# A chunked RWKV-5 attention with a squared-relu FFN on one core: 47 transfers issued by ScalarE's queue, nine transposes moved from DMA to TensorE, and a new order of the steps

## The chip, the core and the metric

The kernel runs on one core of a Trainium2 chip. The core has TensorE (PE, matrix products and transposes into PSUM), VectorE (DVE), ScalarE (ACT), GpSimd (POOL) and SyncE (SP), each with an instruction queue of its own that it works off in order, and 16 DMA engines that the queues of SyncE, ScalarE and GpSimd hand transfers to. The metric is the device time of one execution in microseconds, the median of several runs.

## The reference

```python
B, H, S, D = 4, 8, 768, 48
state = zeros((B, H, D, D))
for t in range(S):
    cur = einsum('bhd,bhe->bhde', u[None] * k[:, :, t], v[:, :, t])
    y[:, :, t] = einsum('bhd,bhde->bhe', r[:, :, t], state + cur)
    state = w[None, :, :, None] * state + einsum('bhd,bhe->bhde', k[:, :, t], v[:, :, t])
x = y.transpose(0, 2, 1, 3).reshape(B * S, H * D)      # 3072 x 384
h = maximum(x @ w_in, 0)                               # 3072 x 2048
return h * h @ w_out                                   # 3072 x 384
```

Everything is fp32 outside; the kernel multiplies in bf16.

## The kernel before

The recurrence is done in chunks of 128 tokens. A unit is one batch and one chunk, all eight heads together: 4 x 6 = 24 units, numbered in the order in which they are worked. For one unit the steps are, by the names that the order uses:

- `ld.r`, `ld.k`, `ld.v` (L312): load r, k, v, 128 tokens x 384 numbers of fp32. The first four units are paired: `lp` (L316) loads two units at once, each row of the tile two neighbouring tokens.
- `rh`, `kh` (L335, L332): multiply r and k by powers of w (tables `Wt`, `Wk`, made once from w) into the bf16 tile `rk`.
- r and k transposed, so that tokens lie along the free dimension (tile `rkT`): either by TensorE (`T`, L393, eight transposes into a PSUM bank, then the copy `Tc`) or by a DMA transpose (`XB`, L399). For the paired units TensorE does it (`TK`, `TR`, copies `KC`, `RC`).
- `A` (L406, paired `Ap` L379): scores of k against r; `Bm` (L414, paired `Bp`): times the causal mask.
- `P0`, `P1`, `du`, `dv` (L338, L342, L345, L350): the term of the token itself, sum over d of r k u, times v. `vb` casts v to bf16.
- `U` (L458): k times v, the chunk's share of the state; `ts` adds it to the old state and `S` (L479) scales by the decay (`S0` for the first chunk).
- `Y` (L445, L447; paired L423 to L435): r times the state plus masked scores times v; `xs` (L470) adds `dv`: this is x of the unit, 128 x 384 bf16.
- x transposed (tile `xT`): by TensorE (`X`, L484, three transposes into PSUM, then the copy `xTc`) or by a DMA transpose (`xX`, L491).

The FFN then runs over groups, units 0 and 1 alone and after that two units at a time (13 groups). `F1.g.s` (L500) is one bank of h of group g (6 matmuls for a group of two units, 12 for a group of one), `re` (L508 on ScalarE, L510 on VectorE) the relu into bf16, `sq` (L515, L517) the square. `F2.i.q` (L526) adds four of the 16 slices of d_ff to unit i's output bank; `os` (L256, L258) brings the bank to SBUF and `out` (L554, L556) stores it. `Z.n` (L535) are n columns-blocks of products of the identity with itself into a spare bank, which nothing reads; four blocks go into one matmul. `lW` and `W` load w_in and w_out, `cW` casts w_in.

The order of all steps is written out by hand as a string, `ORDER`. A step reads `name.unit:engine/slots`, the engine being P (TensorE), D (VectorE), A (ScalarE), G (GpSimd) or S (SyncE's queue, for transfers). Each engine receives its steps in that order and works them off in that order; a buffer's slot is given behind the slash, and the waits between engines follow from tiles and slots. So a transfer that is listed behind another on the same queue is issued behind it, and a wait holds up what is queued behind it. In the kernel before, all loads of r, k, v and all stores are on SyncE's queue, together with the 34 DMA transposes; ScalarE's queue issues only w, u and the two small column loads `wc`.

Of the kernel before, what the change touches and what calls it, by code (L numbers as in the profile page):

```python
# [26 lines left out]
Z.23:P/2 Ap.0.1:P/2/3 dv.1:G vb.2:A/2 WLcol:A du.0:D/1 TK.1:P/4 KC.1:A/2 Bp.0.1.1:D/0 Ap.0.0:P/5/6 rh.3:G/3  # L27
Bp.0.1.0:D/1 Bp.0.0.0:D/2 U.3:P/7 WLm:G vb.1:A/3 Z.10:P/0 U.0:P/0 cW.1:A rh.2:D/2 dv.0:G Bp.0.0.1:D/3 TR.1:P/1 cW.0:A
U.2:P/4 S0.0:D Y.0:P/3 RC.1:A/3 P0.2:D/2 lW.3:S/0 Y.1:P/2 ld.r.5:S/4 P0.3:G/3 P1.3:G S0.2:D ts.3:D/0 ld.k.5:S/4
xs.0:A/0 X.0:P/5 xs.1:A/1 Ap.1.0:P/6/0 Bp.1.0.1:D/4 xTc.0:A/0 Ap.1.1:P/1/4 cW.2:G cW.3:A X.1:P/7 F1.0.0:P/3 ld.k.4:S/5  # L30
xTc.1:D/1 W.1:G Wt.2:A P1.2:D F1.1.1:P/2 du.3:D/2 cW.5:A cW.4:G F1.1.0:P/5 du.2:D/3 re.1.1:A/0 re.0.0:A/1 Bp.1.0.0:D/5
ld.r.4:S/5 F1.0.1:P/7 dv.3:G Bp.1.1.1:D/6 F1.1.2:P/2 dv.2:G ld.v.5:S/4 re.0.1:A/2 Bp.1.1.0:D/7 F1.0.2:P/3 W.0:G cW.7:D
re.1.2:A/3 Y.2:P/7 cW.6:G re.1.0:D/4 Y.3:P/2 Wk.2:A ld.k.6:S/6 xs.2:A/2 re.0.2:D/5 sq.1.1:D/0 sq.1.0:D/1 W.2:G X.2:P/5
W.3:G F1.0.3:P/7 xs.3:A/3 xTc.2:D/0 sq.0.0:A/2 X.3:P/3 ld.r.6:S/6 F1.1.3:P/2 rh.5:D/4 xTc.3:A/0 re.0.3:A/0 re.1.3:A/4
U.1:P/5 F1.2.6:P/3 ts.1:D/1 P0.5:D/4 sq.0.1:D/3 sq.0.3:A/4 F1.2.3:P/7 kh.5:D/4 P1.5:G F1.2.1:P/2 F1.2.2:P/5 re.2.6:A/1
sq.0.2:A/5 sq.1.3:D/6 rh.4:D/5 S.3:G kh.4:G/5 F2.1.1:P/3 du.5:D/4 F2.1.0:P/3 re.2.3:A/2 P0.4:G/0 P1.4:D re.2.1:A/0
re.2.2:A/5 F2.0.0:P/7 ld.v.4:S/5 F1.2.0:P/2 sq.1.2:A/7 F2.0.1:P/7 T.5:P/5 Tc.5:D/4 sq.2.6:A/8 sq.2.3:A/9 F2.1.2:P/3
re.2.0:A/4 sq.2.2:A/10 sq.2.0:A/11 dv.5:G vb.5:G/4 sq.2.1:A/12 du.4:D/0 ld.r.9:S/7 ld.k.8:S/7 F2.0.2:P/7 F2.1.3:P/3
ld.r.7:S/0 kh.6:G/6 F2.0.3:P/7 os.1:A/0 ld.v.6:S/6 ld.k.7:S/0 rh.6:G/6 P0.6:G/1 A.5:P/5/2 os.0:A/1 T.4:P/3 Bm.5.1:D/0
F1.2.4:P/7 Tc.4:A/5 Bm.5.0:D/1 F1.2.7:P/2 ld.k.9:S/1 re.2.4:D/3 P1.6:G A.4:P/3/5 re.2.7:A/1 vb.4:A/5 ld.r.8:S/1  # L40
F1.2.5:P/7 Bm.4.0:D/2 Bm.4.1:D/3 dv.4:G sq.2.7:A/13 Y.5:P/2 F2.2.0:P/3 XB.6:S/6 re.2.5:D/2 U.5:P/5 sq.2.4:A/14
F2.2.1:P/3 ld.k.11:S/2 S0.5:D kh.8:G/2 rh.7:G/3 sq.2.5:A/15 Y.4:P/7 xs.5:D/4 U.4:P/5 ld.v.7:S/7 xs.4:D/0 F2.2.3:P/3
rh.9:G/0 du.6:D/1 X.5:P/2 X.4:P/7 F2.2.2:P/3 xTc.5:A/1 xTc.4:D/1 F1.3.3:P/2 dv.6:G S0.4:D F1.3.4:P/7 os.2:D/2 kh.7:D/3
P0.8:D/3 P1.8:D re.3.4:A/5 F1.3.5:P/5 re.3.3:A/4 re.3.5:A/0 F1.3.2:P/3 re.3.2:A/1 kh.9:D/0 XB.7:S/0 ld.r.10:S/2
out.1:S F1.3.7:P/7 F1.3.6:P/2 P0.7:D/2 F2.3.2:P/5 ld.v.8:S/0 re.3.7:D/3 re.3.6:A/2 sq.3.5:D/16 P1.7:G ld.r.11:S/3
F1.3.1:P/3 vb.6:A/6 S.1:D sq.3.6:A/17 sq.3.3:A/18 ld.v.9:S/1 ld.k.10:S/3 sq.3.2:A/19 A.6:P/7/2 Bm.6.0:D/0 re.3.1:A/0
F2.3.3:P/5 Bm.6.1:D/1 F2.3.1:P/5 XB.9:S/1 F1.3.0:P/7 kh.11:D/1 du.7:D/2 dv.7:G A.7:P/3/2 re.3.0:A/2 sq.3.1:D/20
F2.3.0:P/5 Bm.7.0:D/2 Bm.7.1:D/3 sq.3.0:A/21 F2.4.1:P/7 rh.8:G/2 vb.7:A/7 os.3:D/3 U.6:P/3 sq.3.4:A/22 F2.4.0:P/7
# [72 lines left out]
def kernel(  # L121
# [13 lines left out]
    B, H, S, D = r.shape  # L135
# [124 lines left out]
    class Do:  # L260
# [286 lines left out]
        def out(e, i):  # L547
# [3 lines left out]
            if i < PAIRED:  # L551
                rows = rows.rearrange("(p a) o -> a p o", a=2)
                for a in range(2):
                    e.dma_start(out=rows[a], in_=t[64 * a : 64 * a + 64])  # L554
            else:
                e.dma_start(out=rows, in_=t)  # L556
# [50 lines left out]
```

## Time and profile before

| | |
|---|---|
| median of 3 runs | 178.21 us (177.16 to 178.28) |
| the profiled execution | 179.5 us |
| its span (first to last instruction) | 177.7 us |
| TensorE busy | 164.6 us, 1744 matmuls and transposes, at full granted clock |
| VectorE, ScalarE, GpSimd busy | 136.6, 104.2, 96.3 us |
| DMA, hardware queue | 99424 packets, 28.32 MB, 73.1% of 16 engines' span |
| DMA, software queue (w_out) | 1088 packets, 1.57 MB, 5.1% |
| median issue to landing | r 3.8 us, k 4.2, v 3.7; stores 2.2 (halves of paired ones 2.5); transposes of r, k 4.5, of x 2.9 |
| mean of one instruction | F1 264 ns, F2 326 ns (overlapping; four F2 in a row take 0.65 us); relu 596 ns on ScalarE and 685 on VectorE |

The busy time of an engine leaves out the instructions that issue transfers; these stand in the timeline as a queue's own rows (SPq, ACTq, POOLq). Matmuls are pipelined, so their mean durations are longer than their share of the time; the chain of waits has the time between starts. A wait is put down to what came last. The times of rows are from one execution, 1.3 us above the median.

### The profile page before, as it was taken

The page shows a single profiled execution, that of the slowest core. Times are in us where ns is not written, and L with a number is a line of the kernel's source. Part 1 is how long each engine was busy: PE and PEld are TensorE (multiplying, and loading weights), DVE is VectorE, ACT ScalarE, POOL GpSimd, SP SyncE. Part 2 cuts the span into 40 slices and gives each one's busy share as a digit, 9 for nine tenths or more (in the row PEclk, how much of TensorE's full clock was granted, in tenths as well). Part 3 has the DMA queues.
Part 4 walks back from the last instruction along what each step waited for, and adds up shares of the span by engine and source line. Part 5 has one row for each costly group of instructions (what it writes and reads, how often), then busy time and mean ns, then how long its engine had stood idle before and what let it go on. Part 6 is the DMA issues. An engine that isn't in the chain of part 4 may idle for free.

```text
span 177.7 us, 4457 instructions
## 1 busy us (share of the span) xinstructions
PE 164.6 (93%) x1744; PEld 120.7 (68%) x1744; DVE 136.6 (77%) x251; ACT 104.2 (59%) x195; POOL 96.3 (54%) x118
## 2 busy tenths in 40 slices
PE   4999999999999999797998998997969999999992
PEld 1366988677867785576766776774757878876660
DVE  4789898869997898995779989699977896355020
ACT  2669879774784485086791158792374632677311
POOL 6279975799246396622096979777879300000000
PEclk9999999999999999999999999999999999999999
DMA  5996999899999997768998788999797812110033
GB/s 148 317 378 235 281 226 190 154 200 179 185 209 160 197 195 162 158 130 183 223 212 165 143 163 191 230 220 137 191 171 162 224 23 68 68 44 0 0 133 135
DMA packets 100964, 30.18 MB, mean 170 GB/s; under 512 B 95304, under 2 KB 99408, under 8 KB 100944
## 3 DMA queue, kind: packets, MB, share of 16 engines
q1 hardware_dynamic: 99424, 28.32, 73.1%
q0 software_dynamic: 1088, 1.57, 5.1%
q8 instruction: 13, 0.21, 0.5%
q10 hardware_dynamic: 432, 0.01, 0.2%
q14 instruction: 7, 0.06, 0.1%
HBM read 20.46 MB, written 4.72 MB: 142 GB/s over the span
## 4 chain that ended last, share of the span: by engine, by line
PE 65%; DMA 11%; issue 8%; POOL 8%; ACT 2%; SPq 2%; DVE 2%; POOLq 0%; ACTq 0%
PE bank L526 26%; PE bank L500 24%; DMA rkT<-rk 9%; PE bank L535 4%; PE bank L406 3%; POOL rk L335 2%; DMA ldr<-in_r_dram 2%; PE bank L458 2%; SPq L312 2%; POOL dv L350 2%; POOL rk L332 1%; POOL vb L258 1%; PE bank L435 1%; PE bank L447 1%; PE bank L484 1%
## 5 line engine op out<-in xcount | busy, mean ns | idle before, releaser
L500 PE MATMUL bank<-xT,W 128*128 128x256 bf16 (+1 forms) x624 | 70.0, 264 | 3.4 <-DMA xT<-xs 3.4
L526 PE MATMUL bank<-W,hq 128*128 128x384 bf16 x384 | 70.2, 326 | 0.0
L500 PEld LDWEIGHTS <-W 128*128 128x128 bf16 x624 | 55.6, 98 | 12.3 <-DMA xT<-xs 2.8
L508 ACT ACTIVATE hr<-bank 128x512 bf16<-128x512 f32 x72 | 40.8, 596 | 30.0 <-PE bank L500 25.6
L526 PEld LDWEIGHTS <-hq 128*128 128x128 bf16 x384 | 35.9, 98 | 20.1
L515 ACT ACTIVATE hq<-hr 128x512 bf16<-128x512 bf16 x68 | 40.0, 627 | 3.4 <-DVE hr L510 3.1
L414 DVE TENSOR_TENSOR Bm<-bank,maskJT 128x512 bf16<-128x512 f32 x40 | 26.2, 681 | 6.8 <-PE bank L406 6.8
L342 POOL TENSOR_TENSOR P<-P,ub 128x384 f32<-128x384 f32 x17 | 18.2, 1079 | 13.8 <-DVE P L338 13.5
L256 ACT COPY os<-bank 128x384 f32<-128x384 f32 x16 | 7.6, 475 | 25.6 <-PE bank L526 23.6
L510 DVE TENSOR_SCALAR hr<-bank 128x512 bf16<-128x512 f32 x24 | 16.3, 685 | 6.7 <-PE bank L500 3.5
L335 POOL TENSOR_TENSOR rk<-ldr,Wt 128x384 bf16<-128x384 f32 x15 | 15.3, 1030 | 10.9 <-DMA ldr<-in_r_dram 7.7
L350 POOL TENSOR_TENSOR dv<-ldv,du 128x384 f32<-128x384 f32 (+1 forms) x19 | 16.7, 886 | 5.0 <-DVE du L345 3.6
L517 DVE TENSOR_TENSOR hq<-hr 128x512 bf16<-128x512 bf16 x28 | 15.1, 552 | 2.7 <-ACT hr L508 2.6
L332 POOL TENSOR_TENSOR rk<-ldk,Wk 128x384 bf16<-128x384 f32 x11 | 12.6, 1145 | 1.9 <-DMA ldk<-in_k_dram 1.9
L470 DVE TENSOR_TENSOR xs<-bank,dv 128x384 bf16<-128x384 f32 x20 | 10.8, 550 | 3.0 <-PE bank L447 1.5
L345 DVE TENSOR_REDUCE du<-P 128x8 f32<-128x384 f32 x24 | 12.7, 542 | 0.1
L258 POOL CAST vb<-ldv 128x384 bf16<-128x384 f32 x13 | 7.2, 567 | 9.1 <-DMA ldv<-in_v_dram 9.1
L338 POOL TENSOR_TENSOR P<-ldr,ldk 128x384 f32<-128x384 f32 x9 | 10.3, 1142 | 2.9 <-DMA ldk<-in_k_dram 1.6
L535 PE MATMUL bank<-identity 128*128 128x512 bf16 (+1 forms) x32 | 9.4, 458 | 2.7 <-POOL identity masks.py:199 2.7
L476 DVE TENSOR_TENSOR ts<-bank,S0W 128x384 f32<-128x384 f32 x16 | 8.8, 550 | 2.5 <-PE bank L458 1.4
L332 DVE TENSOR_TENSOR rk<-ldk,Wk 128x384 bf16<-128x384 f32 x13 | 9.7, 752 | 1.1 <-DMA ldk<-in_k_dram 0.5
L406 PE MATMUL bank<-rkT 48*128 48x128 bf16 x160 | 7.3, 218 | 3.4 <-DMA rkT<-rk 3.4
(71 smaller groups left out, 165.5 us busy)
## 6 DMA issues: line engine op xcount, KB each, us to landing
ldr<-in_r_dram SPq DMA_DIRECT2D x20, 192.0 KB, 3.8
ldk<-in_k_dram SPq DMA_DIRECT2D x20, 192.0 KB, 4.2
ldv<-in_v_dram SPq DMA_DIRECT2D x20, 192.0 KB, 3.7
out_dram<-os SPq DMA_DIRECT2D x20, 192.0 KB, 2.2
ws<-in_moe_w_in_dram SPq DMA_DIRECT2D x4, 768.0 KB, 6.7
W<-in_moe_w_out_dram POOLq DMA_DIRECT2D x4, 384.0 KB, 7.0
ldr<-in_r_dram SPq DMA_DIRECT2D x2, 384.0 KB, 4.3
ldk<-in_k_dram SPq DMA_DIRECT2D x2, 384.0 KB, 4.5
```

The source lines that it names most:

```text
L332: e.tensor_mul(rk[slot[f"rk{i}"]][:, 1, :, 0:D], loaded("k", i), Wk[:, i % 2 if i < PAIRED else 0])
L335: e.tensor_mul(rk[slot[f"rk{i}"]][:, 0, :, 0:D], loaded("r", i), Wt[:, i % 2 if i < PAIRED else 0])
L342: e.tensor_mul(t, t, ub)
L350: e.tensor_mul(dv_of(i) if i < PAIRED else dvb[slot[f"dv{i}"]], loaded("v", i), t)
L414: e.tensor_mul(Bmb[slot[f"Bm{i}{h}"]], heads(bank(f"bA{i}{h}"), 128), mask_b)
L500: e.matmul(hp[:, fi, :], W1[f // 2][:, c, 128 * (f % 2) : 128 * (f % 2 + 1)], xt[:, c, :], start=(c == 0), stop=(c == CCH - 1), skip_group ...
L508: e.activation(hr, hp, AF.Relu)
L510: e.tensor_scalar_max(hr, hp, 0.0)
L515: e.activation(hq, hr, AF.Square)
L517: e.tensor_mul(hq, hr, hr)
L526: e.matmul(bank(f"bO{i}")[:, 0:d_model], hqb[slot[f"hq{g},{f // m}"]][:, at : at + L], W2[q][:, f % 4, :], start=(seen[i] == 1 and f % 4 = ...
L535: e.matmul(bank("bZ")[:, 0 : 128 * m].rearrange("p (a b) -> p a b", a=m), identity, bass.AP(tensor=identity.tensor, offset=identity.offset ...
```

## The change

The string of the order is replaced as a whole. 942 steps become 951; which ones differ, and which engine they are on, counted over the whole order (before, after):

| step | before | after |
|---|---|---|
| `ld` | 60 on SyncE | 30 on SyncE, 30 on ScalarE |
| `lp` | 6 on SyncE | 3 on SyncE, 3 on ScalarE |
| `out` | 24 on SyncE | 10 on SyncE, 14 on ScalarE |
| `u` | ScalarE | SyncE |
| `XB` / `T` with `Tc` | 18 / 2 | 17 / 3 (unit 6 moves to TensorE) |
| `xX` / `X` with `xTc` | 16 / 8 | 8 / 16 (units 8, 10, 12, ... 22 move to TensorE) |
| `Z` | 80, 23, 10 | 65, 2, 16 |
| `KC`, `RC` | 4 on ScalarE | 3 on VectorE, 1 on ScalarE |
| `kh` | VectorE 13, GpSimd 11 | 7, 17 |
| `rh` | VectorE 9, GpSimd 15 | 11, 13 |
| `P0` | VectorE 15, GpSimd 9 | 12, 12 |
| `P1` | VectorE 7, GpSimd 17 | 10, 14 |
| `dv` | VectorE 5, GpSimd 19 | 4, 20 |
| `S` | VectorE 9, GpSimd 7 | 3, 13 |
| `vb` | ScalarE 11, GpSimd 13 | ScalarE 12, GpSimd 8, VectorE 4 |
| `re` | ScalarE 72, VectorE 24 | 68, 28 |
| `sq` | ScalarE 68, VectorE 28 | 64, 32 |
| `xs` | VectorE 20, ScalarE 4 | 22, 2 |
| `xTc` | ScalarE 5, VectorE 3 | 11, 5 |
| `cW` | ScalarE 4, VectorE 1, GpSimd 3 | 4, 0, 4 |

The number of matmuls of the products themselves, the slots and the buffers are the same. The places of many steps in the order differ as well, so that the units and groups are interleaved in another way. The store of a paired unit becomes one transfer. The diff, with the beginning, one stretch and the end of the order:

```diff
 ORDER = """
-w:A lp.r.0:S/0 lp.k.0:S/0 lp.v.0:S/0 lp.k.1:S/1 u:A mP.0:G tab:A mJ:G shw:D logw:A lp.v.1:S/1 lp.r.1:S/1 shu:D Wk.1:A
-P0.1:D/0 Wt.1:A lW.0:S/0 kh.1:D/0 Wk.0:A kh.0:D/1 rh.1:G/0 Wt.0:A wc.0:A rh.0:D/1 lW.1:S/1 wc.1:A lW.2:S/2 Z.80:P/0
-TK.0:P/0 P0.0:D/1 P1.0:G vb.0:A/0 TR.0:P/1 KC.0:A/0 P1.1:D du.1:D/0 kh.2:D/2 RC.0:A/1 mP.1:G kh.3:D/3 vb.3:A/1
...
+lp.r.0:A/0 lp.k.0:S/0 mP.0:G u:S shu:D w:A shw:D lp.v.1:A/0 lp.r.1:S/1 lp.v.0:S/1 lW.1:S/0 lW.0:S/1 P0.1:D/0 P1.1:D
+P0.0:G/1 P1.0:D du.0:D/0 tab:A mP.1:G lp.k.1:A/1 du.1:D/1 logw:A Wt.1:A rh.1:G/0 lW.2:S/2 Wk.0:A Wt.0:A kh.2:G/1
+rh.0:D/2 Wk.1:A kh.1:D/0 kh.0:D/2 wc.1:A wc.0:A Z.65:P/0 TR.0:P/0 RC.0:D/0 Z.2:P/1 TK.0:P/1 KC.0:D/1 vb.3:A/0 vb.0:A/1
+vb.1:A/2 U.0:P/2 Ap.0.0:P/3/4 rh.3:G/3 WLcol:A rh.2:G/1 WLm:G Ap.0.1:P/5/6 Wk.2:A vb.2:A/3 kh.3:D/3 U.2:P/7 ld.k.4:A/4
+Bp.0.0.1:D/0 cW.3:A U.1:P/0 ld.r.5:A/4 cW.2:A cW.0:A Bp.0.0.0:D/1 Bp.0.1.0:D/2 Bp.0.1.1:D/3 S0.0:D TR.1:P/1 RC.1:A/2
...
+vb.7:G/7 du.7:D/2 A.7:P/4/5 Bm.7.0:D/2 Bm.7.1:D/3 F1.3.7:P/3 re.3.7:A/4 out.3:A F2.5.1:P/1 F2.4.1:P/0 Y.6:P/7 out.0:A
+U.7:P/4 rh.9:D/3 XB.9:S/2 S.3:D P0.9:D/1 Y.7:P/5 F2.4.2:P/0 dv.7:G xs.7:D/1 P1.9:G U.6:P/3 xs.6:D/2 ld.v.11:A/0
+sq.3.7:A/23 X.7:P/5 xTc.7:A/2 F2.4.0:P/0 ts.7:D/1 ts.6:D/0 X.6:P/7 A.8:P/5/4 Bm.8.1:D/0 ld.k.13:S/4 rh.10:D/4
+kh.10:G/4 XB.10:S/4 F2.5.3:P/1 vb.9:A/1 xTc.6:A/2 F1.4.4:P/3 P0.10:G/2 P1.10:G F1.4.2:P/4 ld.k.12:A/6 Bm.8.0:D/1
+vb.8:G/2 re.4.4:A/0 re.4.2:A/1 ld.k.14:S/7 F1.4.1:P/7 re.4.1:A/3 ld.v.10:A/1 du.9:D/3 A.9:P/5/3 Bm.9.0:D/2 Bm.9.1:D/3
...
+F2.22.1:P/2 F2.22.0:P/2 F2.22.2:P/2 out.17:A F2.18.0:P/0 os.18:D/0 F2.19.0:P/3 F2.19.3:P/3 sq.12.6:A/15 F2.22.3:P/2
+F2.19.1:P/3 out.18:S F2.23.2:P/4 os.19:A/1 out.19:S os.22:D/3 out.22:A F2.23.3:P/4 os.23:A/2 out.23:S
 """
...
             t = osb[slot[f"os{i}"]]
             if i < PAIRED:
                 rows = rows.rearrange("(p a) o -> a p o", a=2)
-                for a in range(2):
-                    e.dma_start(out=rows[a], in_=t[64 * a : 64 * a + 64])
-            else:
-                e.dma_start(out=rows, in_=t)
+            e.dma_start(out=rows, in_=t)
```

More of the change, by code (lines that the diff above doesn't have):

```diff
@@ L29 @@
[L29 to L48, printed above, removed]
@@ new lines @@
+ld.r.6:A/1 sq.2.7:A/10 F2.1.0:P/4 Y.4:P/0 xs.4:D/4 F2.0.2:P/7 F2.1.2:P/4 ld.k.8:S/1 kh.7:G/0 rh.11:G/6 XB.11:S/6
+A.5:P/1/0 sq.2.4:D/11 Bm.5.1:D/2 F2.1.3:P/4 F2.0.3:P/7 sq.2.3:A/12 os.1:A/0 F2.2.3:P/0 sq.2.0:A/13 kh.6:G/2
+sq.2.5:A/14 ld.v.6:A/6 P0.8:G/0 Bm.5.0:D/3 Y.5:P/4 xs.5:D/0 P0.7:D/3 X.4:P/1 xTc.4:D/1 F2.2.1:P/0 ld.k.9:A/2
+F2.2.2:P/0 X.5:P/4 xTc.5:D/1 P0.6:D/2 ld.r.13:S/2 ld.r.9:A/3 F2.2.0:P/0 os.2:A/1 rh.8:D/1 U.5:P/1 S0.5:D rh.6:D/2
+sq.0.0:A/15 rh.7:G/0 F1.3.0:P/4 F1.3.1:P/0 re.3.0:A/4 XB.7:S/1 P1.6:D F2.0.0:P/7 os.0:A/2 du.6:D/1 dv.6:G P0.11:G/4
@@ new lines @@
+U.18:P/5 S.16:G F2.16.1:P/0 S.19:G xTc.18:A/2 F1.10.4:P/7 sq.9.7:A/19 Bm.20.1:D/4 du.20:D/3 ts.18:D/0 S.18:G
+Bm.23.1:D/7 ld.v.22:S/7 vb.22:G/7 F1.10.6:P/1 F1.10.0:P/6 re.10.0:A/4 xs.21:D/0 xX.21:S/0 Y.20:P/5 F1.10.7:P/2
+du.23:D/2 dv.20:D P1.22:D F2.16.3:P/0 F2.17.3:P/4 os.16:A/0 xs.20:D/1 X.20:P/6 xTc.20:A/0 F1.10.2:P/3 re.10.2:A/0
+vb.23:G/6 Y.23:P/0 F1.11.6:P/5 dv.23:G xs.23:D/2 xX.23:S/1 F1.10.1:P/6 Y.22:P/3 du.22:D/4 dv.22:G F1.11.4:P/0
+re.11.6:A/1 xs.22:D/3 sq.11.6:D/16 re.10.7:A/5 out.10:A re.10.6:A/2 sq.10.6:D/17 sq.10.7:D/10 F1.11.3:P/5 re.11.4:D/3
```

126 lines of the change are left out of this document (64 added, 62 removed).

## The prediction

> **What bounds the kernel now.** I read the first part of the page (busy time by engine), then the wait table, then the windows of ten microseconds, and then the timeline of SyncE's queue beside the chain of waits.
>
> ```profile
> PE 164.6 (93%) x1744; PEld 120.7 (68%) x1744; DVE 136.6 (77%) x251; ACT 104.2 (59%) x195; POOL 96.3 (54%) x118
> ```
>
> TensorE leads with 93%; 177.7 - 164.6 = 13.1 us of the span is without a matmul. 2.66 us lie ahead of the first one (the wait for the identity) and 3.3 us behind the last (the chain's last matmul ends at 174.47). Some 7 us are left for the middle. Who caused them is in the wait table (time in total, times, longest):
>
> ```profile
> PE bank L500 <- DMA xT<-xs: 3.4, 3, 1.4
> PE bank L406 <- DMA rkT<-rk: 3.4, 4, 1.5
> ```
>
> So 6.8 us of the middle are two DMA transposes arriving late: x for the first FFN product, and r, k for the scores. The windows (length, busy time of TensorE, its weight load, VectorE, ScalarE, GpSimd, clock, DMA share, GB/s) place them: none between 20 and 70 us, all of them from 70 to 140.
>
> ```profile
> 70.00:80.00 10.00, 8.35 (x95) 6.80 (x93) 9.39 (x17) 4.10 (x9) 4.08 (x4) 1.00 0.74 151
> 80.00:90.00 10.00, 8.77 (x82) 6.77 (x83) 6.65 (x15) 7.20 (x15) 2.37 (x4) 1.00 1.01 211
> ...
> 120.00:130.00 10.00, 8.85 (x103) 6.20 (x101) 9.60 (x18) 3.35 (x7) 8.09 (x8) 1.00 0.89 172
> 130.00:140.00 10.00, 8.51 (x97) 6.83 (x96) 7.55 (x14) 5.88 (x12) 7.75 (x8) 1.00 0.80 172
> ```
>
> Why they are late stands in the timeline of SyncE's queue, 124 to 136 us (start, length, what it issued):
>
> ```profile
> 124.25 0.53 SPq L556 DMA_DIRECT2D out_dram<-os  x1
> 124.83 0.42 SPq L312 DMA_DIRECT2D ldv<-in_v_dram  x1
> 125.31 0.69 SPq L556 DMA_DIRECT2D out_dram<-os  x1
> 126.04 0.43 SPq L312 DMA_DIRECT2D ldv<-in_v_dram  x1
> 126.52 0.72 SPq L312 DMA_DIRECT2D ldk<-in_k_dram  x1
> 127.34 2.27 SPq L399 DMA_TRANSPOSE rkT<-rk  x1
> 129.66 0.58 SPq L312 DMA_DIRECT2D ldr<-in_r_dram  x1
> 130.34 3.31 SPq L491 DMA_TRANSPOSE xT<-xs  x2
> ```
>
> The queue issues without a pause. Summed over this view from 40.8 to 142.1 us it issues for 93.8 of 101.3 us: SyncE's sequencer is the second bound here, and a transpose that is ready stands in line. The chain of waits agrees: one row of the same stretch is
>
> ```profile
> 127.34 5.70 DMA rkT<-rk
> ```
>
> and the matmuls that it frees begin at 133.09.
>
> **The change, part by part.** The base is the profiled execution: 179.5 us, a span of 177.7 and 1.8 around it, 1.3 above the median of 178.2.
>
> SyncE's queue. It issued 132 transfers (60 loads of r, k, v and six paired ones, four of w_in, 28 stores, eight of them halves, 18 + 16 transposes); it keeps 73. Between the same places of the order (the matmul work that the order lists ahead of them runs from 32.5 to 124.5 us) the old order has 45 loads, 18 stores, 18 + 13 transposes on it, the new one 23, 6, 16 + 6. A load is 0.67 us (medians of L312: 0.66 to 0.68), a store 0.56, a transpose of r, k 1.72 and one of x 1.32 on average: 23 x 0.67 + 6 x 0.56 + 16 x 1.72 + 6 x 1.32 = 54 us instead of 93.8. At 54 of 101 us a ready transpose hardly stands in line. Eight of the 16 x transposes, half of the first waiting row, are gone altogether. I take 5.3 of the 6.8 us off, and leave 1.5 for landings that are late for other reasons (bounds 0 and 6.8). What is late next is VectorE (9.4 and 9.6 of 10 us in two windows shown) and the new copies of x.
>
> TensorE. It adds eight transposes of x, 0.17 us each in the chain (L484 x3), and one of r, k, 0.55 (L393 x8): 1.9 us, all of it on the path, since TensorE is the bound. The warm-up products fall from 113 to 83; in the chain they take 7.22, 1.41 (the timeline's x8) and 0.65. 65 columns are 17 products of 0.36 = 6.1, and 2 and 16 are about 1.0, so 7.1 for 9.3: 2.2 us less. They only fill a wait for r, k and the decay tables; with three paired loads now on ScalarE the feed may come earlier, or later as k of the second pair is issued behind a table load of 1.28. I take 1.2 off (bounds 2.2 off, 3 on).
>
> The other engines, counts by row means. VectorE: k scaling -6 x 0.75, r +2 x 0.77, products -3 x 0.65 and +3 x 0.61, states -6 x 0.71, relu +4 x 0.69, squares +4 x 0.55, four casts of v at 0.55, copies of transposed r, k +4 x 0.69, x copies +2 x 0.35, x sums +2 x 0.55, -0.70 and -0.93: +2.7 us, 139 in all. GpSimd: k +6 x 1.15, r -2 x 1.03, products +3 x 1.14 and -3 x 1.08, states +6 x 1.07, casts -5 x 0.57, two more of about 1: +10.5, 107. ScalarE's computing: relu -4, squares -4, copies -3 x 1.01, x copies +6 x 0.48, a cast, two x sums less: -5.4, 99. None passes TensorE; I take 0 for all three, and the price if that cover fails is a rival below.
>
> ScalarE's issues, the added cost. 30 loads x 0.67 + 14 stores x 0.56 + 3 paired loads x 1.15 (SyncE's rows of these) = 31 us, so 99 + 31 = 130 of 178. How it lies beside computing is shown once, in ScalarE's timeline:
>
> ```profile
> 6.08 0.61 ACT L290 ACTIVATE Wk<-logw,njcol 128x384 f32<-128x384 f32 x1
> 6.09 0.86 ACTq L296 DMA_DIRECT2D wcol<-in_w_dram  x2
> 6.60 0.60 ACT L293 ACTIVATE Wt<-logw,tcol 128x384 f32<-128x384 f32 x1
> ```
>
> The sequencer issues while the engine computes, and the next activation isn't late. An activation behind an issue waits only where the engine has run dry. The wait table gives ScalarE 25.6 us before relu on TensorE and 23.6 before evictions: from 70 to 140 us it is busy for 38 of 70, and there the 28 issues that fall between those two places (20 loads, 8 stores, 18 us) cost nothing. Without that cover they cost up to 18. From 10 to 40 us it is busy for 25.8 of 30, and queued behind the loads are the relu and the copies for which TensorE waits: +1.0 (bounds 0 and 9.4, below).
>
> Paired stores. Four transfers for eight take 4 x 0.58 us off a queue; 0 on the path. The tail is as before (last eviction 0.48, issue 0.33, landing); one more store is issued on ScalarE ahead of the last eviction, beside the last four products of 0.65: 0.
>
> Sum: 179.5 - 5.3 + 1.9 - 1.2 + 1.0 = 175.9, against the median 174.6.
>
> **The rivals.** (1) Slower: ScalarE stalls in its own issues early. SyncE's queue between 17 and 35 us shows
>
> ```profile
> 17.35 3.32 SPq L312 DMA_DIRECT2D ldk<-in_k_dram  x2
> 20.72 0.73 SPq L312 DMA_DIRECT2D ldr<-in_r_dram  x1
> 21.49 3.73 SPq L312 DMA_DIRECT2D ldv<-in_v_dram  x1
> ```
>
> and then one of 3.86 at 25.93 and one of 4.61 at 29.84: with the weights in flight (DMA share 0.99 from 10 to 40 us) an issue holds its queue for microseconds. The new order puts eight loads on ScalarE there. If they take as these did (five for 15.5, three at 0.67), that is 17.5 us; 4.2 us of idle time and 4.0 of moved copies cover part, 9.4 are late, and TensorE, without a gap from 20 to 70 us, is late by as much: 174.6 - 1.0 + 9.4 = 183. It decides from 6.4 us late, eight issues over 14.6 us. For it: these rows. Against: two queues share the loads, and the slow ones follow close upon others on one queue.
>
> (2) About the same: the wait passes on. Transposes are freed from the queue, but what feeds them (GpSimd with 10.5 us more, VectorE, or full DMA engines, share 0.93 from 40 to 142 us) is late instead. Nothing of the 6.8 us comes back: 179.5 + 1.9 - 1.2 - 1.3 = 178.9. The Trainium skill ("DMA: Bandwidth & Descriptors", Issuing engines are not separate DMA queues) says that issuing from several engines saves only sequencer time, usually small beside the transfer; by that the time would be this rival's. The trace speaks against "small" here: 93.8 of 101.3 us.
>
> (3) A paired store as one transfer begins, on the DRAM side, with a dimension of two, where each half began with 64 rows. If it is then carried by two of the 16 engines, each moves 64 pieces of 1536 bytes. The mean piece of this queue is 28.32 MB / 99424 = 285 bytes and takes 73.1% x 177.7 x 16 / 99424 = 20.9 ns, so 1536 bytes take up to 113 ns and a store 7.2 us; it landed in 2.5 as halves. Two such stores stand right ahead of the transpose for unit 9 (4.5 us to landing), and the products listed between that and its scores sum to 5.1 us: 4.5 + 7.2 - 5.1 = 6.6 us of stall, 174.6 + 6.6 = 181. The Trainium skill (the same page, Why a DMA increments its semaphore by 16 and not by 1) says so: the number of engines is the largest up to 16 that divides the slowest dimension of both sides. No run here shows it yet.
>
> (4) Faster still: all 6.8 and 2.2 us come back, nothing is lost on ScalarE: 179.5 - 6.8 - 2.2 + 1.9 - 1.3 = 171.
>
> **How the numbers follow.** The forecast gets 0.45, rival 1 0.22, rival 2 0.13, rival 3 0.10, rival 4 0.10. A measurement tells about 1% from no change: 176.4 and 180.0. Rival 4 and all but a little of the forecast's share are below: 0.10 + 0.45 - 0.02 makes faster 0.53. Rival 2, without its upper part of 0.02, and that little are between: 0.13. Slower is the rest, 0.22 + 0.10 + 0.02 = 0.34. The forecast's own range is 171 to 177; the one for 8 in 10 goes from 169 (rival 4, with 2 us of TensorE's shorter stalls that the wait table splits up) to 183.
>
> **What would show it.** Right: SyncE's queue with pauses from 40 to 142 us; the two DMA rows of TensorE's waits under 2 us together; ScalarE's queue rows near 0.6 us. Wrong: ScalarE's issue rows of 2 us and more between 10 and 40 us with TensorE idle there (rival 1); GpSimd or VectorE before the transposes in the chain (2); a landing of 5 us and more for the early stores, and TensorE idle before unit 9's scores (3); a first FFN product later than 19.3 us (the start).

## The result and the profile after

| | before | after |
|---|---|---|
| median of 4 runs each, same chip | 177.84 us (177.16 to 178.28) | 193.18 us (192.18 to 193.53) |
| ratio | | 1.0857 (95%: 1.0799 to 1.0915) |
| the profiled execution, its span | 179.5, 177.7 us | 193.5, 191.8 us |
| first FFN product starts | 19.1 us | 25.0 us |
| last product of TensorE starts | 174.1 us | 186.7 us |

The forecast was 174.6 us, in a range to 183: wrong in sign. Ratios here and below are taken over undisturbed executions, so a median beside one can lie a little higher than the ratio says.

The page's first part, after:

```profile
PE 169.0 (88%) x1767; PEld 123.8 (65%) x1767; DVE 139.7 (73%) x259; ACT 101.3 (53%) x189; POOL 104.3 (54%) x125
```

TensorE does the same products and is still the busiest, but 22.8 us of the span are without a matmul, where before it was 13.1. VectorE, ScalarE and GpSimd came out as counted (139, 99 and 107 forecast). The wait table of TensorE has other rows at its head (time in total, times, longest):

```profile
PE bank L407 <- DMA rkT<-rk: 4.7, 2, 4.5
PE bank L459 <- ACT vb L257: 4.2, 1, 4.2
...
PE bank L501 <- DMA xT<-xs: 0.7, 1, 0.7
```

The row of x fell from 3.4 to 0.7, as forecast. The row of r, k is now one stall of 4.5 us, and a new wait stands at the start, for a cast of v. The windows (length, TensorE, weight load, VectorE, ScalarE, GpSimd, clock, DMA share, GB/s) place both:

```profile
10.00:20.00 10.00, 5.04 (x89) 4.41 (x90) 5.93 (x11) 5.11 (x11) 6.15 (x8) 0.71 0.87 274
20.00:30.00 10.00, 10.00 (x184) 7.67 (x181) 8.42 (x15) 6.18 (x12) 7.83 (x10) 0.95 1.13 243
...
60.00:70.00 10.00, 8.89 (x103) 6.32 (x100) 8.70 (x16) 3.00 (x6) 6.18 (x7) 1.00 0.88 101
70.00:80.00 10.00, 6.62 (x50) 4.89 (x51) 3.81 (x7) 5.31 (x10) 4.97 (x6) 0.66 1.47 158
```

TensorE is half idle from 10 to 20 us and a third idle from 70 to 80, and in both windows its granted clock is low (0.71, 0.66; before it was 1.00 in every window of ten up to 170 us). SyncE's queue, the point of the forecast, does pause now. Its timeline in the stretch shown of before:

```profile
125.88 1.19 SPq L492 DMA_TRANSPOSE xT<-xs  x1
127.12 0.57 SPq L313 DMA_DIRECT2D ldk<-in_k_dram  x1
127.74 0.57 SPq L313 DMA_DIRECT2D ldr<-in_r_dram  x1
128.36 0.73 SPq L554 DMA_DIRECT2D out_dram<-os  x1
129.85 1.23 SPq L400 DMA_TRANSPOSE rkT<-rk  x1
```

Between 40.8 and 142.1 us it issues for 62.8 us, where before it was 93.8.

**Time by stage.** To put the runs beside each other, each step of TensorE gets the time that it takes when nothing is late (from the chain of before: six first-layer products 0.66 us, four second-layer ones 0.65, scores 0.33, an x 0.17 and so on; 159 us in all). The table has, at the point where TensorE has done so much of this work, the time on the profile less the work: how far it has fallen behind. A difference between two columns is what was lost between the two points. The column of 18 moves by up to 1.4 us with the times that one takes for the short early steps, the others by half a microsecond. The profiled executions of e20, e21 and e9 were 3.4, 2.4 and 1.1 us above their medians, which their last column contains.

| behind, us, after so much work | 18 | 48 | 54 | 156 |
|---|---|---|---|---|
| before | 7.0 | 7.2 | 7.4 | 15.2 |
| after | 16.0 | 17.0 | 24.4 | 27.6 |
| e1_split | 17.0 | 17.5 | 19.1 | 19.8 |
| e2_merged | 7.4 | 7.4 | 12.4 | 25.0 |
| e9_loads_first | 13.6 | 14.1 | 15.8 | 16.0 |
| e14_vb_first | 10.3 | 10.3 | 11.9 | 12.6 |
| e17_best | 11.9 | 12.0 | 13.4 | 13.6 |
| e19_best_all_sync | 13.0 | 13.5 | 13.7 | 17.4 |
| e15_x_dma | 14.0 | 14.5 | 16.0 | 27.3 |
| e20_x_dma_early | 14.0 | 14.5 | 16.1 | 29.1 |
| e16_old_order_x_pe | 6.7 | 6.9 | 7.7 | 11.4 |
| e21_old_order_x_pe_queue | 7.1 | 8.5 | 8.7 | 17.8 |

After against before: the start loses 9.0 us, the stretch around the early stores (48 to 54) 7.2, the stretch 18 to 48 0.8, and the rest gains 4.6. That is 12.4; with 0.2 more work and 1.5 us more between the last product and the end it is the 14.1 us between the spans.

### The profile page after: what moved, and what is told of

Read it like the earlier page. It is cut to its first block, busy times and chain, and to the rows that moved or that the text cites. A ratio compares the mean times of both kernels' runs of the same rounds, so it can differ in the third digit from the quotient of the medians.

```text
span 191.8 us, 4499 instructions
## 1 busy us (share of the span) xinstructions
PE 169.0 (88%) x1767; PEld 123.8 (65%) x1767; DVE 139.7 (73%) x259; ACT 101.3 (53%) x189; POOL 104.3 (54%) x125
## 4 chain that ended last, share of the span: by engine, by line
PE 48%; DMA 30%; POOL 7%; DVE 7%; ACT 3%; issue 2%; ACTq 1%; SPq 0%; POOLq 0%; DVEq 0%
PE bank L501 20%; PE bank L527 19%; DMA rkT<-rk 12%; DMA out_dram<-os 4%; DMA wcol<-in_w_dram 4%; DMA ldr<-in_r_dram 3%; DMA xT<-xs 3%; DMA urow<-in_u_dram 2%; DMA ldk<-in_k_dram 2%; POOL rk L333 2%; DVE Bm L415 2%; POOL P L339 2%; PE bank L407 1%; DVE rk L336 1%; PE bank L459 1%
## 5 line engine op out<-in xcount | busy, mean ns | idle before, releaser
L501 PE MATMUL bank<-xT,W 128*128 128x256 bf16 (+1 forms) x624 | 72.7, 270 | 1.9 <-DMA xT<-xs 0.7
L501 PEld LDWEIGHTS <-W 128*128 128x128 bf16 x624 | 57.0, 100 | 11.7 <-issue 1.5
L509 ACT ACTIVATE hr<-bank 128x512 bf16<-128x512 f32 x68 | 39.1, 595 | 27.3 <-PE bank L501 17.9
L516 ACT ACTIVATE hq<-hr 128x512 bf16<-128x512 bf16 x64 | 37.7, 625 | 5.9 <-DVE hr L511 2.5
L333 POOL TENSOR_TENSOR rk<-ldk,Wk 128x384 bf16<-128x384 f32 x17 | 18.2, 1080 | 13.5 <-DMA ldk<-in_k_dram 13.5
L511 DVE TENSOR_SCALAR hr<-bank 128x512 bf16<-128x512 f32 x28 | 18.8, 683 | 3.5 <-PE bank L501 2.5
L343 POOL TENSOR_TENSOR P<-P,ub 128x384 f32<-128x384 f32 x14 | 14.4, 1036 | 8.9 <-DVE P L339 8.7
L480 POOL TENSOR_TENSOR S0W<-ts,WLm 128x384 bf16<-128x384 f32 x13 | 13.9, 1076 | 3.9 <-DVE ts L477 3.9
L336 POOL TENSOR_TENSOR rk<-ldr,Wt 128x384 bf16<-128x384 f32 x13 | 13.7, 1057 | 2.3 <-DMA ldr<-in_r_dram 2.1
L339 POOL TENSOR_TENSOR P<-ldr,ldk 128x384 f32<-128x384 f32 x12 | 13.1, 1092 | 2.4 <-DMA ldr<-in_r_dram 2.4
L257 ACT COPY xT<-bank 128x384 bf16<-128x384 bf16 x11 | 5.3, 479 | 14.5 <-PE bank L485 14.4
L259 DVE COPY os<-bank 128x384 f32<-128x384 f32 x8 | 4.4, 553 | 11.1 <-PE bank L527 11.1
L459 PE MATMUL bank<-vb,rk 128*128 128x96 bf16 (+1 forms) x96 | 7.4, 217 | 5.1 <-ACT vb L257 4.2
```

Source lines behind the costliest of these rows:

```text
L333: e.tensor_mul(rk[slot[f"rk{i}"]][:, 1, :, 0:D], loaded("k", i), Wk[:, i % 2 if i < PAIRED else 0])
L336: e.tensor_mul(rk[slot[f"rk{i}"]][:, 0, :, 0:D], loaded("r", i), Wt[:, i % 2 if i < PAIRED else 0])
L339: e.tensor_mul(P0b[slot[f"P{i}"]], loaded("r", i), loaded("k", i))
L343: e.tensor_mul(t, t, ub)
L501: e.matmul(hp[:, fi, :], W1[f // 2][:, c, 128 * (f % 2) : 128 * (f % 2 + 1)], xt[:, c, :], start=(c == 0), stop=(c == CCH - 1), skip_group ...
L509: e.activation(hr, hp, AF.Relu)
```

## The experiments

The orders are cut to the steps that an edit touches.

### The paired store: e1_split, e2_merged

e1_split is the changed kernel with the paired stores in halves again, e2_merged the kernel before with each as one transfer:

```diff
 e1_split
             if i < PAIRED:
                 rows = rows.rearrange("(p a) o -> a p o", a=2)
-            e.dma_start(out=rows, in_=t)
+                for a in range(2):
+                    e.dma_start(out=rows[a], in_=t[64 * a : 64 * a + 64])
+            else:
+                e.dma_start(out=rows, in_=t)
 e2_merged
-                for a in range(2):
-                    e.dma_start(out=rows[a], in_=t[64 * a : 64 * a + 64])
-            else:
-                e.dma_start(out=rows, in_=t)
+            e.dma_start(out=rows, in_=t)
```

> The changed kernel with the paired stores again as two halves of 64 rows; nothing else. Theory (a paired store as one transfer runs on two engines and holds up what shares them): the lag that TensorE picks up between 48 and 54 us of its own work (7.4 us in the changed kernel, 0.2 in the one before) goes, the transpose for unit 9 lands within 5 us instead of 10.4, and the time is 185 to 187 us. Rival (two queues filling the DMA engines at once make that stall): 192 to 194 us, the stall stays.

> The kernel before with the paired stores as one transfer each; nothing else. Theory (two engines): each such store lands 6 us and more after its issue instead of 2.5, transposes behind it on SyncE's queue land 5 us and more later than 4.5, and the time is 181 to 185 us. Rival (the stores are harmless, four issues of 0.58 us saved): 176.5 to 178 us.

e1_split: 184.33 us beside 180.51, ratio 1.0226 (1.0131 to 1.0321), where the whole change has 1.0857. e2_merged: 190.07, ratio 1.0544 (1.0448 to 1.0641). So four stores as one transfer each cost 6% in the new order and 5% in the old one, 9 to 11 us. In the changed kernel the chain of waits shows what they hold up:

```profile
62.92 10.40 DMA rkT<-rk
...
73.38 0.61 PE bank L407 x8
73.98 2.03 PE bank L501 x9
```

and ScalarE's timeline of the same stretch shows what was issued ahead of that transpose:

```profile
61.85 1.17 ACTq L554 DMA_DIRECT2D out_dram<-os  x2
...
65.94 5.18 ACTq L313 DMA_DIRECT2D ldk<-in_k_dram  x1
```

A transpose of r, k, which lands in 4.5 us (at most 5.7) before, takes 10.40 behind two paired stores, and a load's issue takes 5.18 us where all other loads of one unit but one, of 2.7, take 0.4 to 1.0. The DMA packets in the traces, counted by how many pieces of a store (1536 bytes) are in flight together, show why:

```
kernel      stores  pieces   first to last      in flight together
before      1       128      57.9 to 58.9 us    14 or more for 0.65 of 0.97 us
e2_merged   1       128      60.0 to 65.1 us    2 for 4.5 of 5.1 us
after       2       256      63.1 to 73.5 us    2 for 8.5 of 10.4 us
```

As one transfer a store goes out two pieces at a time, as two halves fourteen and more for two thirds of its time. The rule that the prediction named as a rival (the Trainium skill, "DMA: Bandwidth & Descriptors", Why a DMA increments its semaphore by 16 and not by 1) gives two engines here, and these counts agree with it. With two such stores under way the count stays at two, so they take turns on the same two engines, and the transpose issued among them landed 0.2 us before their last piece. In the old order the stall has another face. The chain of e2_merged:

```profile
58.79 6.64 DMA out_dram<-os
...
65.51 0.49 ACT os L256
```

and its wait table, all engines:

```profile
ACT os L256 <- DMA out_dram<-os: 10.5, 3, 7.7
```

Here the next eviction waits for the store's buffer, three times, 10.5 us in all. The expectation had 181 to 185 us and transposes that land late: its mechanism for the store holds, but the transposes whose landing the trace has came in 5.8 us at most, and the wait that made 190 was not in it.

### The start: e3, e4, e9 to e14, e17

With the stores split 10 us are still lost by the end of 18 us of work. ScalarE's timeline of the changed kernel has the head of it (the bracket: idle time before it, and who ended it):

```profile
7.12 0.52 ACT L278 ACTIVATE logw<-wb 128x384 f32<-128x384 f32 x1 [2.88 <-DVE wb L272]
...
9.04 0.32 ACTq L297 DMA_DIRECT2D wcol<-in_w_dram  x1
...
16.00 0.20 ACT L300 ACTIVATE wcol<-wcol 128x4 f32<-128x4 f32 x1 [4.82 <-DMA wcol<-in_w_dram]
...
16.86 0.49 ACT L257 CAST vb<-ldv 128x384 bf16<-128x384 f32 x1
```

and GpSimd's the second feed, k of the second pair:

```profile
13.71 1.30 POOL L333 TENSOR_TENSOR rk<-ldk,Wk 128x384 bf16<-128x384 f32 x1 [4.17 <-DMA ldk<-in_k_dram]
```

Three holds can be read off: the table of w begins 1.6 us later than before (7.12 for 5.52), since on VectorE the shuffle of u, whose load lands at 6.0, now stands ahead of that of w; k of the second pair is issued by ScalarE beside w_in's 768 KB loads and lands at 13.6; and the cast of v of unit 2 is queued behind a step that waits for a column load of 0.8 KB, which took 6.9 us to land (3.3 before). The edits:

```diff
 e3_wc_early (on after), e4_both (the same on e1_split)
-w:A shw:D lp.v.1:A/0
+w:A shw:D wc.1:A wc.0:A lp.v.1:A/0
...
-wc.1:A wc.0:A Z.65:P/0
+Z.65:P/0
 e9_loads_first (on e1_split)
-lp.v.1:A/0 lp.r.1:S/1 lp.v.0:S/1 lW.1:S/0
+lp.v.1:S/0 lp.r.1:S/1 lp.v.0:S/1 lp.k.1:S/1 lW.1:S/0
...
-lp.k.1:A/1
 e10_w_first (on e1_split); e11_start_both is e9 and e10 together
-lp.r.0:A/0 lp.k.0:S/0 mP.0:G u:S shu:D w:A shw:D
+w:A lp.r.0:A/0 lp.k.0:S/0 mP.0:G shw:D shu:D u:A
 e13_shw_first (on e9)
-u:S shu:D w:A shw:D
+u:S w:A shw:D shu:D
 e14_vb_first (on e9); e17_best is e13 and e14 together
-rh.3:G/3 WLcol:A rh.2:G/1 WLm:G Ap.0.1:P/5/6 Wk.2:A vb.2:A/3
+rh.3:G/3 vb.2:A/3 WLcol:A rh.2:G/1 WLm:G Ap.0.1:P/5/6 Wk.2:A
```

e10_w_first, e11_start_both and, further down, e12_all_sync leave out the term of u: its shuffle reads the row ahead of u's load. The load of u, on ScalarE's queue in them, waits for that shuffle instead.

> The changed kernel with the two small column loads of w issued ahead of the paired loads of v and k on ScalarE's queue; nothing else. Theory (the column loads stand behind 1024 pieces of the paired load of k in ScalarE's own transfers, ScalarE's queue then waits for them, and with it the cast of v for the third state product): they land within 4 us instead of 6.9, the 4.2 us wait of TensorE on that cast goes, and the time is 185 to 189 us. Rival (the paired load of k itself comes too late, 13.7 us, and holds the same products): TensorE waits on k's scaling instead, 191 to 193 us.

> Both edits. If both theories hold and the two stalls do not hide each other: 193.2 - 7 - 6 = 178 to 182 us. If only the stores count: 185 to 187. If neither: 192 to 194.

e3_wc_early: 195.37 us, ratio 1.0832 (1.0745 to 1.0919), the same as the change; e4_both: 186.56, 1.0366 (1.0289 to 1.0443), no better than e1_split and probably worse. The wait for the columns was gone, and ScalarE waited 5.34 us for v of the second pair in its place, until 16.03. The paired loads of v and k, now issued at 6.20 and 7.49, among or behind w_in's first three (3.44 to 6.63), are there at 16 to 17 us.

> The changed kernel with the stores split (the base from here on, 184.3 us beside 180.5 of the kernel before) and its two paired loads of the second pair, v and k, issued by SyncE ahead of the w_in loads. Theory A (these loads share the DMA engines with 768 KB pieces of w_in that overtake them, and the scaling of k waits for them until 13.7 us): k lands before 10.5 us, the start's lag of 17 us at 18 us of TensorE's own work falls by 4 to 8, time 177 to 181 (beside 180.5). Theory B (the decay tables are late, since the shuffle of w stands behind that of u, 1.6 us): less than 2 us gained, 182.5 to 184.5.

> The base with w issued first on ScalarE's queue, u second, and the shuffle of w ahead of that of u, as in the kernel before; the paired loads stay where the change put them. Theory B: log w starts at 5.5 us as before instead of 7.1 and the time falls by 1.6 to 5 us, 179.5 to 183. Theory A: the start still waits for k, 183.5 to 185.

> Both edits of the start on the base. If A and B are both needed: the lag at 18 us of TensorE's own work comes to 7 to 9 us as in the kernel before, and the time to 173 to 177, faster than the kernel before (180.5) by 2 to 4%, because the waits of the middle are shorter. If something else in the new start's order holds it (the transposed r ahead of k, the casts' places): 178 to 184.

e9_loads_first: 180.64 us beside 178.8; its four runs lie between 176.6 and 181.8, too far apart for a ratio. Its profile shows the mechanism: k is there at 11.14 for 13.71, the wait for the columns is 2.6 us for 4.8, and the start is 3.4 us shorter than that of e1_split (13.6 for 17.0). e10_w_first: 185.83, 1.0407 (1.0364 to 1.0449), slower than e1_split. It doesn't test what it was made for. ScalarE stood in the load of u until the shuffle was done (issued at 6.25 us), so the logarithm of w, which was to start at 5.5 us, began at 8.61 (7.12 in the changed kernel), k of the second pair was issued at 7.80 and the first r came 2 us later. e11_start_both: 183.6, 1.0277 (1.0225 to 1.0329): the same hold (the logarithm at 8.03) outweighs the gain of e9.

> e9_loads_first with the shuffle of w ahead of the shuffle of u on VectorE, nothing else (the edit of e10_w_first also moved the load of r and put u's shuffle ahead of its load, so that it left out u's term and delayed the table load; this one does not). Theory B: log w at 5.6 us instead of 7.1, the transposed r, k 1 to 1.5 us earlier, the start's lag of 13.6 us down by 1.5 to 3, time 1.5 to 3 us under e9_loads_first's 180.6. Rival (the start is held by what comes after, the column load and ScalarE's wait for it): within 1 us of it.

> e9_loads_first with the fourth cast of v ahead of the step on ScalarE that waits for w's columns, nothing else. Theory (ScalarE's queue stands 2.6 us before the column load and holds the cast for the third state product): TensorE's 1.8 us wait on that cast goes, lag down by 1 to 2 us. Rival (the product is then held by k's scaling at 13.5 us, and the casts of w_in stay behind the wait): less than 1 us.

> The split stores, v and k of the second pair on SyncE's queue ahead of w_in, the shuffle of w ahead of that of u, and the cast of v of unit 2 ahead of the step that waits for the column loads, together. If the start is made of these three holds: TensorE's late start relative to its work falls to 9 or 10 us by 18 us of work (16.0 in the changed kernel, 10.3 with the cast alone moved) and the time is 174 to 176, ratio 0.97 to 0.985. If one feed remains behind all of them (the landing of k): as e14, 176.5 to 178, ratio 0.987.

e13_shw_first: 180.36 us, ratio 0.9904 (0.9832 to 0.9975). Its logarithm begins at 6.26 us (7.08 in e9), but by the median it is 0.3 us ahead of e9 and by 48 us of work 0.4: the side of its rival. e14_vb_first: 178.3, 0.9867 (0.9772 to 0.9963). The wait of TensorE for the cast of v, in the timelines of the changed kernel, of e9 and of e14 (a fence each):

```profile
17.40 1.10 PE L459 MATMUL bank<-vb,rk 64*128 64x96 bf16 x16 [4.17 <-ACT vb L257]
```

```profile
15.01 0.99 PE L459 MATMUL bank<-vb,rk 64*128 64x96 bf16 x16 [1.83 <-ACT vb L257]
```

```profile
13.48 0.91 PE L459 MATMUL bank<-vb,rk 64*128 64x96 bf16 x16
```

The same sixteen products start 3.9 us earlier than in the changed kernel, and nothing ahead of them waits; the granted clock of the whole run is 1.00, where e1_split has 0.97. e17_best: 178.22, 0.9889 (0.984 to 0.9939), no better than e14: 11.9 us behind where the expectation had 9 or 10. The two holds don't add: in e13 too the cast is earlier, and these products start at 13.23. A start of 3 to 5 us later than before stays: TensorE waits 1.47 us for the scaled r at 9.97, and from 10 to 20 us its granted clock is 0.83. What holds that rest no run took away.

### The middle: x by DMA again, and x by TensorE in the old order

e1_split loses 2.8 us from 18 to 156 us of work where before loses 8.2: the gain of 5.4 us that the prediction had put at 5.3. What brings it was tried from both sides.

```diff
 e15_x_dma (on e9; the same for x of units 10, 12, ... 22), at the place of X
-X.8:P/7 xTc.8:A/0
+xX.8:S/0
 e20_x_dma_early (on e15; where xX stood later)
-xs.8:D/4 ld.r.14:A/4
+xs.8:D/4 xX.8:S/0 ld.r.14:A/4
 e16_old_order_x_pe (on before; the same for units 10, 12, ... 22)
-xs.8:D/3 xX.8:S/0 Y.9:P/5
+xs.8:D/3 Y.9:P/5
...
-F2.6.0:P/2 du.11:D/0
+F2.6.0:P/2 X.8:P/3 xTc.8:A/0 du.11:D/0
```

> e9_loads_first with the eight x that the change gave to TensorE back on DMA transposes from SyncE's queue, at the places of the TensorE transposes; the transfers stay divided between the two queues. Theory (SyncE's queue made the waits): SyncE has room, so no wait comes back; 1.4 us less work on TensorE, time within -1.5 to +1 us of e9_loads_first. Rival (the x by TensorE are what shortened the middle, since a DMA transpose of x needs 4 us): the first FFN products wait 3 to 5 us more in total, +3 to +5.

> e15 (eight x by DMA again in the new order, 191.3 us) with each of the eight DMA transposes right behind the sum that makes x, where e15 had it at TensorE's place, 1 to 15 steps later. If e15's 11 us are the late place of the issue: within 3 us of e9 (177 to 181). If they are the DMA transpose itself (its latency and its slot in the queue, against products that the new order puts close behind): 186 us or more, with TensorE still waiting for xT for 5 us or more.

> The kernel before in its own order, paired stores in halves, but the eight x of units 8, 10, ... 22 are transposed by TensorE into the unit's own Y bank, two TensorE steps behind the place of the DMA transpose, and copied by ScalarE. If the middle's gain is that x no longer waits for a DMA: TensorE's rows of waiting for xT (3.4 us before) fall below 1, eight x of 0.17 us add 1.4, the copies lie in ScalarE's idle time, and the time is 1 to 3 us under the kernel before on the same chip. If the gain is the order as a whole: within 1% of the kernel before or slower, with TensorE waiting for the copies of x in place of the transposes.

e15_x_dma: 191.29 us, ratio 1.0663 (1.0539 to 1.0787); e20_x_dma_early: 188.84, 1.0423 (1.0353 to 1.0492). Back on the DMA, the eight x cost the new order 8 to 11 us over e9's median (180.6; its fastest run was 176.6), 2 to 4 us less where they are issued as early as can be. TensorE's wait tables, of e15 and of e20:

```profile
PE bank L501 <- DMA xT<-xs: 7.3, 4, 4.0
```

```profile
PE bank L501 <- DMA xT<-xs: 7.1, 2, 6.1
```

and the chain at e20's longest:

```profile
104.20 0.03 SPq L492
...
104.27 4.54 DMA xT<-xs
...
108.86 4.00 PE bank L501 x18
```

The queue isn't what holds it there: the issue follows at once, then 4.54 us go by to the landing, and the 18 products behind it take 4.00 us, twice their usual time, at a granted clock of 0.66 in that window. Further up the same chain stands a load of v that took 7.46 us to land, so x was late as well as slow. SyncE's queue is as relieved in e15 (60.8 us of the 101.3) as in the changed kernel.

e16_old_order_x_pe: 176.98 us (176.9 to 177.07) beside 179.66, ratio 0.9853 (0.9812 to 0.9894): the lowest ratio of the study, though not apart from e14's, in the old order with the old start. Its wait table of TensorE:

```profile
PE bank L536 <- POOL identity masks.py:199: 2.7, 1, 2.7
PE bank L501 <- ACT xT L257: 1.1, 2, 0.6
PE bank L459 <- ACT xT L257: 0.6, 1, 0.6
PE bank L446 <- ACT xT L257: 0.6, 1, 0.6
PE bank L407 <- ACT xT L257: 0.4, 1, 0.4
PE bank L485 <- DVE xs L471: 0.4, 1, 0.4
...
```

Two rows of 0.4 and 0.3 for the first r, k are left out. No DMA stands in it, neither x nor r, k, though only x was taken off the DMA and SyncE's queue still issues for 80.3 of the 101.3 us. The transposes of r, k land in 3.8 us in the median, for 4.5 before. In place of 6.8 us of DMA waits stand 2.7 of waits for the copies of x. From 18 to 156 us of work it loses 4.7 us for 8.2, and has 1.4 us more work.

### The queue alone: e6, e12, e19, e21

```diff
 e6_old_order_two_queues (on before, 32 times: 18 loads, 14 stores); e21_old_order_x_pe_queue (the same 32 on e16)
-ld.v.8:S/0
+ld.v.8:A/0
...
-out.1:S
+out.1:A
 e12_all_sync (on e11), e19_best_all_sync (on e17): 45 and 44 loads and stores
-ld.k.4:A/4
+ld.k.4:S/4
...
-out.3:A
+out.3:S
```

> The kernel before, its order and transposes unchanged, with 32 loads and stores that stand after the first product of group 3 moved from SyncE's to ScalarE's queue at their places (the ones that the change moved too). Theory (SyncE's queue is the bound of the middle): the 8 us of lag between 54 and 126 us of TensorE's work shrink by 4 to 6, time 173 to 175 beside 178.8. Rival (the order and the transposes make the middle, as e12_all_sync hints with 1.3 us between the queues): 177 to 179. Third: ScalarE's issues hold relu and evictions: over 180.

> As e11_start_both, but the other 45 transfers that the change put on ScalarE's queue go back to SyncE's, at the same places of the order: the queue alone. Theory (SyncE's queue is the bound of the middle): SyncE issues for over 85 of the 101 us from 40 to 142, waits of TensorE on transposes come back, and the time is 3 to 6 us above e11_start_both. Rival (the middle is easier because the transposes stand earlier in the new order and eight of x are gone): within 1.5 us of it.

> e17 with the 44 loads and stores on ScalarE's queue back on SyncE's, at the same places of the order. If SyncE's relieved queue carries the middle's gain, as predicted: 3 to 6 us above e17, with TensorE's waits for DMA transposes up by as much. If the queue hardly matters once eight x have left the DMA: within 1.5 us of e17.

> e16 (old order, eight x by TensorE, 177.0 us, ratio 0.985) with 32 later loads and stores moved from SyncE's to ScalarE's queue, the part of the change that alone brought 0.6% in the old order. If the two parts cure different waits: ratio 0.978 to 0.982. If both cure the same wait, x and r, k late from DMA, of which e16 shows no row over 0.3 us any more: 0.983 to 0.988, as e16.

| pair | SyncE's queue, 40.8 to 142.1 us | ratio to before |
|---|---|---|
| before, e6 (some moved) | 93.8, 76.5 | 1, 0.9942 (0.989 to 0.9993) |
| e16, e21 (some moved) | 80.3, 55.5 | 0.9853, 1.024 (1.0184 to 1.0297) |
| e12 (all on SyncE), e11 | 82.0, 57.2 | 1.0351 (1.0282 to 1.042), 1.0277 |
| e19 (all on SyncE), e17 | 80.7, 58.1 | 1.0044 (1.0002 to 1.0086), 0.9889 |

The relieved queue is worth 0.6% in the old order, 0.7% (less than the intervals) and 1.5% in the new one, and it costs 3.9% once x of the old order is on TensorE: 181.1 us, beside 177.42 on that chip, which fits neither side of the expectation. The chain of e21 where it falls behind most, and rows of its wait table, all engines:

```profile
89.82 6.65 DMA rkT<-rk
...
96.52 0.40 PE bank L407 x8
```

```profile
POOL rk L336 <- DMA ldr<-in_r_dram: 5.4, 1, 5.4
...
PE bank L407 <- ACT hr L509: 1.8, 3, 1.0
...
PE bank L407 <- DMA rkT<-rk: 1.6, 1, 1.6
```

SyncE's queue is free, the transpose is issued as soon as GpSimd has scaled r, k, and takes 6.65 us to land; GpSimd itself had waited 5.4 us for r. All four pairs have this in common: with two queues the transposes of r, k take longer from issue to landing, in the median 4.9 us for 4.5 (e6 for before), 4.2 for 3.8 (e21, e16), 4.2 for 3.5 (e11, e12) and 4.2 for 3.2 (e17, e19). So part of what an earlier issue gains is given back on the way. The Trainium skill ("DMA: Bandwidth & Descriptors", Issuing engines are not separate DMA queues) has transfers of all issuing engines run on the same DMA engines, so that only the issue's own time is saved; these medians agree. Another part is paid on ScalarE. In e6 TensorE's DMA waits fall from 6.8 to 4.6 us, and 2.7 us of waits for ScalarE's relu appear, of which before has none (e6's profiled execution was 2.1 us above its median). The chain of e6 shows one:

```profile
47.21 1.01 POOL P L342
48.22 0.04 ACTq L312
...
48.37 0.61 ACT hr L508
```

By this chain a load of v on ScalarE's queue waits for the end of GpSimd's product, and the relu queued behind the load starts only then, after 1.80 us in which ScalarE computes nothing; the scores that wait for this relu follow at 49.01. On SyncE's queue such a wait holds up transfers alone. Why all this ends in a gain of 1 to 3 us in three pairs and in a loss of 4 in the fourth isn't settled: ScalarE has eight copies more in e21, and the relu is in its wait table too, but no run separates the two.

## Why the prediction was wrong, point by point

- **Paired stores: the step that failed first.** "Four transfers for eight take 4 x 0.58 us off a queue; 0 on the path." They cost 6% (1.0857 for 1.0226) and 5.4% in the old order. Rival 3 named the mechanism, the place (the transpose for unit 9 behind two stores) and 11.7 us to its landing; measured were 10.4, and the sign that it gave came, 4.5 us of TensorE idle before unit 9's scores. Its 7.2 us per store came from 113 ns a piece; a store took 5.1, 80 ns a piece. The 9.2 us between the spans of the change and of e1_split are, by stage, 5.8 at this place (7.4 lost for 1.6; 6.6 worked out), 2.5 later on, where the chain has the fourth store with 7.02 us from 95.19, and 1.4 behind the last product, less 0.5 in which the change happened to be ahead by then. The rival had counted the first place alone. The mistake was the weight: a rule with a mechanism and a place in this kernel got 0.10, as nothing in the trace of before could show it.
- **The start: "I take 1.2 off (bounds 2.2 off, 3 on)".** It was 9.0 us later by 18 us of work, outside the bounds. The prediction looked at the table load ahead of the issue of k; the issue was early enough (3.0 us), but the transfer landed beside w_in only at 13.6. The wait of the cast of v behind the column loads (3.3 us, e14) and the shuffle of u ahead of that of w (0.4 us, e13) were in the order's first lines and were not read for it. "A first FFN product later than 19.3 us" was among the signs, and came: 25.0.
- **The middle: -5.3 for TensorE's DMA waits.** In size right (5.4 with the stores in halves), but by luck, for the cause was wrong in the larger part. The step "at 54 of 101 us a ready transpose hardly stands in line" put it down to SyncE's queue. The queue was relieved as counted (62.8 us; 58.5 with halves; 54 forecast), but moving the issues alone gave 0.6% in the old order, while eight x by TensorE, with the queue at 80.3 us, took every DMA row out of the wait table and made 1.5%. In the new order the queue does count: from 18 to 156 us of work e17 loses 1.7 us and e19, all on SyncE, 4.4, so 2.7 of the 6.5 us gained on before come with it; with the eight x back on the DMA, e15 loses 10.9 us more there than e9. A busy queue was there, but it was not the main thing that set the end.
- **Nine more transposes, +1.9.** Right as far as it was tested: eight of them are 1.4 us of work in e16, and its 4.7 us lost for 8.2 pays for them.
- **ScalarE's issues, +1.0, and rival 1.** Its rows of loads and stores are 0.3 to 1.0 us but for two, of 5.18 and 2.7, and the longer one stands beside the paired stores; with halves none is over 1.2 us. No early stall of ScalarE in its own issues was seen; what it waited for early were landings. Rival 1 fell. "An activation behind an issue waits only where the engine has run dry" doesn't hold where the load must wait for its buffer, as e6 shows.
- **Rival 2, the wait passes on:** at the very point of change it didn't (x 3.4 to 0.7, in e1_split r, k 3.4 to 0.3), but the pairs on the queue show its kind: landings grow by 0.4 to 1.0 us.

With the stores in halves, the loads of the second pair ahead of w_in and the cast moved, the new order runs at 0.987 to 0.989 of before. For e14 the stages add up so: 3.3 us lost at the start, 5.9 gained behind it, 0.2 of more work, 2.4 us gained in all, where the forecast had 3.6.

## What to carry to other kernels

Before joining two transfers into one, look at the outer dimension that each side then begins with: with a 2 in front a 192 KB store went out on two pieces at a time, took 5.1 us for 1.0, and held up the transposes and loads issued beside it or the eviction that needed its buffer. A queue that issues without a pause is a suspect, not a bound: take one waiting transfer away and see whether the wait goes, before all of the queue's work is moved. A load that moves to a computing engine's queue takes its wait for a buffer along, and the computing behind it waits too. And in the first 20 us a load's place against the weights decides when it lands, so read each step that waits there for what is queued behind it.

## What the runs showed of the hardware

- Where TensorE had idled for 4 to 6 us, the granted clock was 0.66 to 0.71 in the window with the end of the stall (10 to 20 and 70 to 80 us of the changed kernel; 105 to 115 of e20_x_dma_early): nine first-layer products took 2.03 us where six take 0.66. So the stall of 4.5 us before unit 9's scores cost 7.4 us by the table of stages. In e14_vb_first, without the idle time at the start, the mean clock is 1.00, in e1_split 0.97.
- A column load of 0.8 KB issued behind w_in's first three loads took 6.9 us to land (6.5 in e12_all_sync, without a paired load ahead of it on its queue), and 3.3 us in the kernel before, where it was issued ahead of them: size said nothing there.
- While two paired stores were under way (60 to 70 us), the DMA engines moved 101 GB/s at a busy share of 0.88. From 40 to 50 us, without a paired store, 104 GB/s took a share of 0.53.
